# Sixty-four extra TensorE steps put into the order of a fused RWKV-7 and SwiGLU kernel

## The chip, the cores and the metric

The kernel runs on one core of one Trainium2 chip. The metric is device time in microseconds (us). A core has five instruction streams that run beside each other: PE (TensorE: matrix products; its weight loads are shown as PEld), DVE (VectorE), ACT (ScalarE), POOL (GpSimd) and SP (SyncE, which here only issues DMAs). Each executes its own instructions in order; they wait for each other by semaphores. The profile also shows the TensorE clock that was granted at each moment, as a share of full speed.

## What is computed

The reference is a recurrence followed by a feed-forward block. The recurrence runs over 768 steps in 4 batches of 8 heads, each with a state of 40x40; its output, seen as 3072 rows of 320 numbers, goes through an RMS norm and a SwiGLU block of inner size 1536. The weights of the block come as 64-bit floats.

```python
for t in range(S):
    y[:, :, t] = np.einsum('bhd,bhde->bhe', rt, state)
    Sa = np.einsum('bhde,bhe->bhd', state, at)
    state_decay = state * wt[:, :, None, :] - np.einsum('bhd,bhe->bhde', Sa, bt)
    state = state_decay + np.einsum('bhd,bhe->bhde', vt, kt)
x = y.transpose(0, 2, 1, 3).reshape(B * S, H * D)
rms = np.sqrt(np.mean(x * x, axis=-1, keepdims=True) + 1e-06)
xn = x / rms * rms_g
g = xn @ w_gate
out = (g * (1.0 / (1.0 + np.exp(-g))) * (xn @ w_val)) @ w_out
```

## The kernel before

The 768 steps are cut into 24 chunks of 32. For each chunk there are three stages. `front` loads r, w, k, v, a and b, turns them with TensorE transposes against the identity matrix `ident` (tiles wan and kbn are the inputs of such turns), scales them by decay products (T, K, A, Ab, KN) and makes the chunk's triangular matrix LT by products of A or Ab with K, out of which DVE picks elements with masks. `inverse` sends LT through memory (sB, then M; SP issues these DMAs), inverts it on DVE in a chain of small steps on Yi and tmp, and sends the result back (sY, LT). `main` solves for the chunk's updates (Xs, LT, and in the first five chunks also LB), copies them to VU, updates the state ST, and makes the output y from scores (rE, vut) and five levels of products (As, KN). Its rows are normed (ss, x) and turned once more into xg.

Chunks are gathered in 13 groups, the first and last of one chunk, the others of two. `feed` runs the feed-forward block for a group: products of xg with the weight tiles wf, Silu into sg, hT, and products with the output weights that are summed up in the PSUM tile po, columns 0 to 319 of each of its two banks of 512. Before the first group, `narrow` turns the 64-bit weights into 32-bit ones: DMAs issued mostly by POOL bring the raw halves into wf, and some steps on DVE and ACT (tiles exs, ex, o) make floats of them. All of this narrowing lies in the first fifth of the run, beside the first chunks.

The code doesn't issue instructions as it goes. It records each operation, or each group of products, as a piece of a `Plan`. `Plan.issue` then goes through a list of words, ORDER, written out by hand in the file: each word is an offset from the first piece not yet issued, and names the piece that is issued next. All engines' queues, the DMA queues among them, follow from that one list. A second list, PAIRS, says which of three PSUM tiles (ps) each intermediate uses. Waits are set from the overlaps of what pieces write and read.

Since helpers issue everything, many operations share a line: 469 is a group of products, 472 a group of transposes, 423 a DVE operation, 446, 450 and 453 ACT operations (activation, copy, scaling), 462 a POOL fill, 466 a DMA, 982 and 986 steps of the narrowing.

Of the kernel before, what the change touches and what calls it, by code (L numbers as in the profile page):

```python
# [16 lines left out]
P = 128  # L17
# [325 lines left out]
def kernel(  # L343
# [660 lines left out]
    for c in range(-2, NCH):  # L1004
# [5 lines left out]
        if c + 2 < NCH:  # L1010
            front(c + 2)
            inverse(c + 2)

    plan.tc = tc
    with tc.manual_schedule():
        plan.issue(ORDER, PAIRS)

# [29 lines left out]
```

## Time and profile before

| what | value |
|---|---|
| median of 3 runs | 1022.03 us (1021.31 to 1022.28) |
| the profiled execution | 1018.8 us |
| its span, first to last instruction | 1017.0 us |
| PE busy | 925.3 us (91%) |
| DVE busy | 771.2 us (76%) |
| ACT busy | 509.7 us (50%) |
| POOL busy | 350.8 us (34%) |
| mean granted TensorE clock | 0.944 |

A busy share is the time in which at least one instruction of the engine runs. In a timeline row stand the start, the length, the engine, the line, the operation, the tile written and the tiles read, the shape as rows*columns of the array part used, the size of the operand, and the count; in brackets the idle time of the engine before it and what ended that. A product is recorded as two instructions (32 products of a group are x64), a transpose as one.

### The profile page before, as it was taken

To read this page: it belongs to the slowest core of one execution; us is meant where nothing else is said; L and a number is where in the kernel's file an instruction comes from. 1 tells how busy PE (TensorE), PEld (TensorE's weight loads), DVE (VectorE), ACT (ScalarE), POOL (GpSimd) and SP (SyncE) were. 2 spreads that over 40 slices of the span, in tenths; PEclk is the share of its full clock that TensorE was granted. 3 is DMA by queue.
4 is the path that set the end of the run, shared out by engine and by line. 5 is a ranking of instruction groups with operands and counts; after the bars stand their busy time and mean duration, and the time that the engine had idled before them with its cause. 6 is when DMAs were issued, how large, how long until landed. Compare 5 with 4: busy or idle time off the path is not lost.

```text
span 1017.0 us, 55373 instructions
## 1 busy us (share of the span) xinstructions
PE 925.3 (91%) x24512; PEld 758.6 (75%) x24512; DVE 771.2 (76%) x2718; ACT 509.7 (50%) x1133; POOL 350.8 (34%) x595
## 2 busy tenths in 40 slices
PE   4367678999999999999899999999999999999998
PEld 4256667877877877788678778877877777777877
DVE  8888887786967966976869779779689688685531
ACT  6787477455455545354453454444545545435131
POOL 8988353233133314314233143243234134210000
PEclk9556767999999999999999999999999999999999
DMA  8674453323234323223142142232232232310100
GB/s 171 150 188 115 99 111 76 64 46 70 39 70 75 59 53 77 49 59 73 18 95 45 43 87 47 60 80 45 59 76 51 61 62 52 72 33 9 42 6 20
DMA packets 140175, 68.87 MB, mean 68 GB/s; under 512 B 120768, under 2 KB 127264, under 8 KB 139936
## 3 DMA queue, kind: packets, MB, share of 16 engines
q0 software_dynamic: 19680, 32.48, 15.9%
q1 hardware_dynamic: 118080, 32.54, 15.6%
q8 instruction: 192, 3.15, 1.3%
q10 hardware_dynamic: 2176, 0.33, 0.2%
q14 instruction: 47, 0.39, 0.1%
HBM read 55.05 MB, written 10.22 MB: 64 GB/s over the span
## 4 chain that ended last, share of the span: by engine, by line
PE 58%; DVE 16%; DMA 7%; issue 7%; POOL 5%; ACT 4%; SPq 3%; DVEq 0%; ACTq 0%; POOLq 0%
PE ps L469 42%; PE po L469 10%; PE ps L472 5%; DVE Yi L423 3%; SPq L466 3%; DVE tmp L423 2%; DMA M<-sB 2%; DVE K L423 2%; DVE y L423 2%; DMA sB<-LT 2%; POOL kbn L466 2%; DVE As L423 1%; DVE LT L423 1%; POOL wf L466 1%; DMA LT<-sY 1%
## 5 line engine op out<-in xcount | busy, mean ns | idle before, releaser
L469 PE MATMUL ps<-xg,wf 128*128 128x256 f32 (+3 forms) x1872 | 360.2, 374 | 1.6 <-ACT sg L446 0.6
L469 PEld LDWEIGHTS ps<-xg,wf 128*128 128x128 f32 (+1 forms) x1872 | 267.9, 189 | 47.9 <-issue 7.1
L469 PE MATMUL po<-wf,hT 128*128 128x320 f32 x576 | 178.6, 443 | 0.0
L469 PEld LDWEIGHTS po<-wf,hT 128*128 128x128 f32 x576 | 104.2, 190 | 35.3 <-issue 1.6
L423 DVE TENSOR_TENSOR tmp<-Yi,M 128x24 f32<-128x24 f32 (+21 forms) x512 | 107.2, 209 | 13.7 <-DMA M<-sB 2.7
L423 DVE TENSOR_TENSOR Yi<-Yi,tmp 128x24 f32<-128x24 f32 (+21 forms) x512 | 107.0, 209 | 10.7
L423 DVE TENSOR_TENSOR hT<-ps,sg 128x256 f32<-128x256 f32 (+1 forms) x156 | 60.8, 399 | 70.5 <-PE ps L469 42.6
L466 POOL DMA_DIRECT2D kbn<-in_k_dram x92 | 54.4, 593 | 148.8 <-PE ps L469 147.9
L446 ACT ACTIVATE sg<-ps 128x256 f32<-128x256 f32 (+1 forms) x156 | 54.0, 367 | 82.8 <-PE ps L469 82.3
L423 DVE TENSOR_TENSOR K<-K,T 128x256 f32<-128x256 f32 (+1 forms) x191 | 94.4, 505 | 1.1 <-PE ps L469 0.2
L423 DVE SCALAR_TENSOR_TENSOR Yi<-M,Yi 128x27 f32<-128x27 f32 (+6 forms) x228 | 44.6, 244 | 66.1 <-DMA M<-sB 51.8
L466 POOL DMA_DIRECT2D kbn<-in_b_dram x92 | 53.8, 587 | 118.4 <-PE ps L469 117.4
L469 PE MATMUL ps<-Ab,K 64*60 64x56 f32 (+2 forms) x4608 | 80.4, 226 | 14.7 <-ACT r L450 4.8
L469 PEld LDWEIGHTS ps<-Ab,K 64*60 64x60 f32 (+2 forms) x4608 | 73.6, 138 | 25.6 <-issue 5.9
L450 ACT COPY KN<-ps 128x640 f32<-128x640 f32 x95 | 65.5, 692 | 52.1 <-PE ps L472 20.4
L466 POOL DMA_DIRECT2D VU<-in_v_dram x92 | 53.8, 588 | 104.6 <-PE ps L469 103.5
L423 DVE TENSOR_TENSOR As<-ps,msi 128x256 f32<-128x256 f32 (+1 forms) x168 | 72.0, 456 | 16.5 <-PE ps L469 9.3
L469 PEld LDWEIGHTS ps<-As,KN 128*40 128x40 f32 x3072 | 65.8, 127 | 16.7 <-ACT As L453 4.5
L469 PE MATMUL ps<-As,KN 128*40 128x32 f32 x3072 | 70.1, 207 | 7.5 <-DVE As L423 4.4
L466 POOL DMA_DIRECT2D wn<-in_w_dram x92 | 53.0, 578 | 62.4 <-DVE KN L423 39.3
L456 POOL TENSOR_TENSOR ss<-ss,mhalf 128x1 f32<-128x1 f32 x24 | 17.5, 728 | 163.7 <-DVE ss L423 160.8
L450 ACT COPY K<-K 128x512 f32<-128x512 f32 x95 | 60.4, 635 | 21.2 <-PE ps L469 10.9
(137 smaller groups left out, 1530.8 us busy)
## 6 DMA issues: line engine op xcount, KB each, us to landing
M<-sB SPq DMA_DIRECT2D x96, 128.0 KB, 2.8
wan<-in_r_dram SPq DMA_DIRECT2D x24, 160.0 KB, 3.8
kbn<-in_b_dram POOLq DMA_DIRECT2D x92, 40.0 KB, 2.7
VU<-in_v_dram POOLq DMA_DIRECT2D x92, 40.0 KB, 2.8
wan<-in_w_dram POOLq DMA_DIRECT2D x46, 80.0 KB, 3.1
wan<-in_a_dram POOLq DMA_DIRECT2D x46, 80.0 KB, 2.7
kbn<-in_k_dram POOLq DMA_DIRECT2D x92, 40.0 KB, 2.3
wn<-in_w_dram POOLq DMA_DIRECT2D x92, 40.0 KB, 2.7
```

The costliest lines, as they stand in the source:

```text
L423: plan.add("DVE", time + more + each * size(o), 0.087, lambda at: [fn(at(o), *m(at))], [o], aps(*args))
L446: scalar(o, [a], lambda at: nc.scalar.activation(at(o), at(a), f, **kw), aps(acc), 0.1 if f in (AF.Square, AF.Relu) else 0.0)
L450: scalar(o, [a], lambda at: nc.scalar.copy(at(o), at(a)), extra=more)
L456: plan.add("POOL", 0.5, 0.06, lambda at: nc.gpsimd.tensor_tensor(o, a, b, op), [o], [a, b])
L466: plan.add(by, 0.6 if by == "POOL" else 0.45, 0.0, lambda at: queue.dma_start(out=o, in_=i), [o], [i], load=load, since=since)
L469: return o, lhsT, rhs, lambda at: nc.tensor.matmul(at(o), lhsT, rhs, start=start, stop=stop, skip_group_check=True), 4
L472: return o, i, ident, lambda at: nc.tensor.transpose(at(o), i, ident), 2
```

## The change

64 words "-" are put among the first 1188 of the 5993 words of ORDER; without them the list is the same as before, and so is PAIRS. At each such word `Plan.issue` calls `plan.warm`, which issues four products. Product j takes 32 columns of `ident`, on all 128 rows, as its stationary operand, and 96 columns of `ident`, read twice, as its moving operand. It writes 32 partitions of po, 192 columns behind those that `feed` uses; nobody reads them. The four products write the four quarters of the partitions. They are no pieces of the plan: no order between them and other pieces is recorded beyond what the tiles `ident` and `po` call for.

```diff
@@ ORDER, an extract @@
-35 0 0 0 46 359 380 185 73 0 32 170 171 181
+35 0 0 0 46 359 380 185 - - 73 0 32 170 171 181
...
@@ Plan.issue @@
         for word in order.split():
+            if word == "-":
+                self.warm()
+                continue
             i = first + int(word)
...
@@ end of the kernel function @@
+    plan.warm = lambda: [nc.tensor.matmul(po_[rows(j // 2, j % 2), 1, DM:DM + 192], ident[:, 32 * j:32 * j + 32],
+                                          ident[:, None, 0:96].to_broadcast((P, 2, 96)), skip_group_check=True) for j in range(4)]
     plan.tc = tc
     with tc.manual_schedule():
         plan.issue(ORDER, PAIRS)
```

DM is 320, P is 128, and `rows(i, x)` is the quarter of the partitions that starts at 64 i + 32 x. The words stand alone or in runs of two to six, 37 runs in all counted on PE's queue. On the queues of DVE, ACT, POOL and SP the instructions and their waits are the same as before. On PE the products come between the groups that were there; the wait for the filling of `ident`, which the first transposes had, is now on the first of them.

More of the change, by code (lines that the diff above doesn't have):

```diff
@@ L33 @@
 76 84 83 86 75 71 2 3 4 5 6 7 0 35 47 0 17 54 64 0 0 51 0 35 0 55 0 0 67 68 60 190 191 41 49 374 59 71 375 0
[149 rows of a table removed]
+35 0 0 0 46 359 380 185 - - 73 0 32 170 171 181 75 74 73 0 1 27 3 0 368 2 0 352 373 343 173 2 167 166 342 72 80 73 85 84
+96 - - 69 70 78 83 94 74 365 79 40 53 353 62 371 61 366 354 64 51 52 374 54 81 15 93 75 82 76 92 95 91 367 - 86 89 90 63 183
+77 100 344 168 39 165 297 298 88 104 184 102 106 97 87 105 101 198 108 98 107 348 345 103 185 190 113 99 346 16 656 668 175 176 9 5 31 109 112 368
@@ new lines @@
+355 369 116 114 117 115 118 120 119 110 111 347 186 - 187 122 356 299 359 349 203 370 350 191 657 18 665 4 357 188 197 284 19 17 28 375 121 71 196 376
+667 666 43 382 285 377 358 123 202 379 201 213 30 0 401 171 652 41 199 359 379 198 360 25 - - - 191 123 300 299 210 124 125 126 127 213 128 211 301
+129 192 130 209 - 203 131 193 132 221 208 206 402 392 654 391 382 390 205 133 207 134 181 657 170 5 194 377 223 219 135 222 136 214 217 137 218 138 204 216
+230 393 139 380 225 411 140 141 215 410 413 142 143 226 144 145 383 146 147 148 149 150 151 224 412 234 663 384 235 236 152 385 386 237 168 387 153 155 662 154
@@ new lines @@
+156 394 388 403 389 407 395 404 238 239 240 396 180 414 415 405 406 6 43 318 7 13 433 22 408 398 - - - 676 157 432 179 418 399 419 241 416 397 409
+229 188 158 159 160 161 400 228 417 452 31 453 244 420 441 443 245 246 434 247 248 444 677 227 - - - 242 435 436 243 442 249 220 250 251 252 438 253 254
+464 463 169 437 - - - 285 454 461 0 460 253 254 437 255 453 284 256 438 456 454 - 285 286 287 257 482 0 250 251 435 643 447 252 436 449 473 283 280
+253 254 281 450 282 255 223 493 256 439 257 258 259 260 261 494 651 437 - - - 292 455 438 262 22 662 263 264 440 293 441 456 661 660 1 - 296 475 457
@@ new lines @@
+483 459 479 284 303 458 482 299 460 298 484 285 300 485 461 297 648 665 476 304 302 306 305 222 307 309 477 301 495 310 502 505 650 503 478 664 499 311 221 313
+- 312 266 267 265 268 270 314 504 23 315 486 496 497 763 316 480 271 269 272 764 317 822 821 481 487 498 832 819 676 500 318 488 506 319 490 320 766 544 489
+663 501 669 491 507 - 321 767 322 545 833 768 769 770 536 508 535 829 670 677 323 492 675 682 - 771 820 525 324 671 772 775 510 680 681 773 692 668 774 534
+524 509 325 - - - 778 679 678 693 690 688 672 686 765 689 691 673 687 683 779 828 533 16 2 831 827 674 294 699 694 697 511 700 512 526 701 824 830 834
@@ new lines @@
+649 823 295 698 702 703 685 527 528 705 684 546 695 782 838 658 0 204 370 380 211 378 203 511 333 205 212 215 206 216 389 390 391 228 467 463 462 460 382 213
+381 459 465 464 - - 475 476 214 221 398 222 470 385 383 457 458 388 392 395 393 394 466 461 224 384 469 386 223 217 225 471 450 468 - 474 752 230 451 226
+399 400 401 402 403 404 405 406 407 408 409 410 751 499 249 749 762 759 411 472 412 387 413 473 414 - 517 250 761 - 513 415 477 518 416 417 478 760 418 419
+479 420 421 480 422 423 481 424 425 426 427 482 - 614 615 516 617 510 227 229 509 750 428 629 515 514 - 396 520 429 431 430 630 432 528 521 397 526 527 522
@@ new lines @@
+532 530 529 533 534 523 544 524 531 537 536 541 525 542 538 540 535 543 539 436 434 - 545 549 553 548 0 553 549 434 545 555 432 550 560 546 554 556 565 566
+567 551 558 250 557 230 234 235 518 254 255 231 232 251 - - - - - - 617 564 568 571 570 765 615 618 - 619 233 252 236 559 620 253 770 - 621 453
+569 256 574 771 259 630 257 623 258 260 757 499 575 576 577 578 579 580 581 582 583 584 585 586 587 588 589 590 591 592 593 594 595 596 622 625 624 - - 626
+627 597 598 454 746 632 - - 634 633 747 269 764 635 631 - 0 637 - 481 0 1 0 478 399 669 679 668 515 558 565 555 516 177 670 556 517 518 519 400
@@ new lines @@
+401 181 520 671 178 402 672 564 522 523 521 524 563 562 - 574 557 477 566 182 179 180 403 567 183 561 568 560 559 573 572 569 570 571 575 576 577 578 579 783
+184 844 854 842 841 843 - 784 682 744 684 685 528 525 526 840 678 852 527 786 683 186 580 187 689 479 - - 404 697 488 407 406 489 696 787 188 788 789 688
+690 702 190 849 848 857 405 700 785 713 851 853 839 191 189 701 - - 581 695 790 710 858 791 582 192 850 712 691 583 698 795 584 711 794 724 193 733 709 792
+699 847 793 585 692 194 708 - - 798 196 707 693 799 - 703 195 706 694 723 717 714 719 722 718 704 705 725 715 721 730 0 725 585 715 733 5 196 6 719
@@ new lines @@
+734 7 730 726 1 727 736 0 733 6 198 799 0 194 0 547 798 46 799 194 805 0 730 796 543 719 47 728 190 192 803 729 722 798 42 731 799 806 43 44
+801 805 48 49 802 795 797 804 50 807 0 763 0 763 689 690 691 692 693 694 695 767 765 764 766 686 696 768 697 1067 769 803 687 698 770 - 0 943 942 694
+800 766 695 799 767 41 1075 696 802 697 805 1064 698 48 47 813 806 803 1065 1063 1073 699 818 700 817 42 43 0 768 767 1030 657 757 0 4 769 770 784 657 762
+5 658 774 0 779 658 762 770 780 775 - - 46 782 791 778 659 781 660 763 776 661 53 52 47 49 54 0 43 759 657 772 784 658 769 659 779 783 788 660
[120 rows of a table added]
```

269 rows, old and new, of the table ORDER are left out of this document.

## The prediction

> **What bounds the kernel now.** I read the page first, then the busy time by stretches, then the chain of waits. The page's rows are the span cut into 40 slices of 25.4 us, busy share in tenths; PEclk is the granted TensorE clock.
>
> ```profile
> span 1017.0 us, 55373 instructions
> ...
> PE   4367678999999999999899999999999999999998
> DVE  8888887786967966976869779779689688685531
> POOL 8988353233133314314233143243234134210000
> PEclk9556767999999999999999999999999999999999
> ```
>
> PE is full from the seventh slice on, and there the clock is full too. In the six slices before, PE has idle time, DVE and POOL are nearly full, and the clock is granted at half to three quarters. The busy time by stretches gives the sizes (columns: stretch, length, then PE, PEld, DVE, ACT, POOL busy with instruction counts, granted clock, DMA share, GB/s).
>
> ```profile
> 0.00:57.00 57.00, 22.45 (x705) 20.23 (x706) 50.54 (x157) 39.91 (x71) 51.60 (x95) 0.73 0.75 168
> 57.00:77.00 20.00, 15.04 (x512) 13.76 (x512) 17.04 (x53) 16.21 (x31) 16.18 (x27) 0.50 0.72 173
> 77.00:95.00 18.00, 13.56 (x560) 11.90 (x556) 15.62 (x41) 12.85 (x29) 17.38 (x26) 0.59 0.50 125
> 95.00:112.00 17.00, 10.32 (x439) 9.85 (x432) 14.97 (x46) 10.33 (x19) 9.96 (x18) 0.80 0.48 111
> 112.00:163.00 51.00, 38.46 (x1477) 34.61 (x1478) 41.71 (x135) 33.94 (x76) 26.97 (x46) 0.60 0.46 95
> 163.00:215.00 52.00, 48.08 (x1430) 40.88 (x1426) 39.18 (x145) 29.47 (x68) 13.10 (x23) 1.00 0.34 71
> 215.00:1017.00 802.00, 777.35 (x19411) 627.42 (x19410) 592.12 (x2147) 367.01 (x845) 215.59 (x364) 1.00 0.28 54
> ```
>
> Up to 95 us POOL (51.60 of 57, 16.18 of 20, 17.38 of 18) and DVE (50.54 of 57) set the pace. From 112 to 163 us no engine is full. From 163 us PE is busy 92%, from 215 us 97%: whatever the front part gains or loses stays in the end time one for one. The chain of waits, cut to two stretches, says how much of them is PE:
>
> ```profile
> by line: PE ps L469 49.9%; DMA wf<-in_moe_w_out_dram 23.9%; ACT VU L450 8.2%; ACT exs L446 6.8%; ACT vut L450 5.0%; ACT As L453 4.6%; issue 4.1%; DVE As L423 3.7%; ACT exs L982 3.4%; ACT ST L450 2.8%; ACT Xs L453 2.2%; DVE exs L423 2.1%; AC
> by line: PE ps L469 45.4%; PE ps L472 12.2%; issue 6.6%; ACT KN L450 4.1%; ACT K L450 4.0%; ACT VU L450 3.2%; ACT exs L446 2.5%; DVE LT L423 2.3%; ACT rE L450 2.0%; ACT A L450 1.9%; ACT T L450 1.9%; DVE K L423 1.5%; ACT Xs L453 1.5%; DVE y
> ```
>
> 57 to 77.5 us: 49.9% of 20.5 us, 10.2 us of PE on the chain, all at clock 0.50. 112 to 163 us: 45.4% and 12.2%, 29.4 us of PE. A mean clock of 0.60 there, with only 0.5 and 1.0 granted, means 80% of the time at half: 23.5 us. What half a clock costs is seen in one product group at two times:
>
> ```profile
> 12.02 1.97 PE L469 MATMUL ps<-A,K 64*64 64x56 f32 x64 [1.10 <-DVE Ab L423]
> 186.05 1.15 PE L469 MATMUL ps<-A,K 64*64 64x56 f32 x64
> ```
>
> 1.15 us against 1.97 us: full clock saves 0.42 of such a group. (The first lies in a slice whose PEclk digit reads 9, yet runs at the slow pace; that digit I don't believe before about 20 us.)
>
> What lifts the clock is read from windows of 3.41 us, the step at which the grant changes here (PE busy, then clock):
>
> ```profile
> 84.70:88.11 3.41, 2.52 (x108) 0.50 0.48 118
> 88.11:91.53 3.42, 3.24 (x89) 0.50 0.67 199
> 94.94:98.35 3.41, 3.41 (x144) 0.50 0.40 69
> 98.35:101.77 3.42, 0.72 (x68) 1.00 0.56 103
> 101.77:105.18 3.41, 3.07 (x93) 0.50 0.36 117
> 105.18:108.59 3.41, 3.19 (x155) 1.00 0.52 134
> 115.42:118.83 3.41, 1.66 (x80) 1.00 0.44 77
> 132.49:135.90 3.41, 3.31 (x116) 0.50 0.59 176
> 146.14:149.55 3.41, 2.62 (x135) 1.00 0.54 103
> 149.55:152.97 3.42, 1.94 (x127) 1.00 0.61 123
> ```
>
> At half clock, windows busy 3.41 and 3.07 us were followed by 1.00; one of 2.52 was not, nor were 3.24 (1.50 us of it the transposes of VU at 88.76, shown below) and 3.31. At full clock, windows busy 3.19 and 2.62 us were followed by another full one; 1.94, 1.66 and 0.72 were not. So the bar is about 0.9 of a window to rise and 0.6 to 0.75 to stay.
>
> **The change part by part.** Nothing is removed, and no other instruction moves on DVE, ACT, POOL or SP; none of their waits changes. PE gets 64 steps of 4 products, each a 32-column slice of ident against 192 columns, out to the unused columns of po, in 37 bursts. They wait only once, for ident, ahead of the first transposes, which had that wait before. Nobody waits for them; queued behind them is PE's own next step, and whoever waits for that.
>
> *Price of a step.* A product is two instructions, as 32 products of A,K make the x64 above; so 8 instructions of 192 columns.
>
> ```profile
> L469 PE MATMUL ps<-xg,wf 128*128 128x256 f32 x1056 | 258.0, 388 | 0.5 <-issue 0.4
> L469 PE MATMUL ps<-As,KN 128*40 128x32 f32 x2688 | 57.9, 203 | 2.1 <-ACT As L453 1.3 <-DVE As L423 0.6 <-DVE y L423 0.2
> ```
>
> 258.0 us for 1056 instructions of 256 columns: 0.95 ns a column at full clock, 183 ns for 192 columns. If four column groups run wholly side by side, a step is two instructions long, 0.37 us; if not at all, eight, 1.46 us. As,KN, on all rows with outputs in two column halves, takes 21.5 ns for 32 columns where 0.95 ns a column makes 30.5: column groups do overlap there. I take 0.4 us at full clock and 0.75 us at half, nearest to that row; 1.46 us is kept as a rival.
>
> *Where the steps lie.* By the order of instructions against the timeline: 19 steps before 57 us, 6 from 57 to 77, 5 to 95, 5 to 112, 26 from 112 to 163, 3 after 180 us. Some gaps (start, length, product, idle before it):
>
> ```profile
> 50.88 1.09 PE L472 MATMUL ps<-ident,kbn 64*104 64x64 f32 x16 [8.61 <-POOL kbn L462]
> 63.92 0.34 PE L472 MATMUL ps<-ident,VU 64*104 64x64 f32 x1 [0.97 <-ACT VU L450]
> 88.76 1.50 PE L472 MATMUL ps<-ident,VU 64*104 64x64 f32 x16
> 126.97 1.32 PE L469 MATMUL ps<-Xs,LT 32*32 32x40 f32 x64 [0.44 <-DMA LT<-sY]
> 130.30 1.29 PE L469 MATMUL ps<-Xs,LB 16*32 16x40 f32 x64 [2.01 <-ACT Xs L450]
> 136.89 1.10 PE L472 MATMUL ps<-ident,VU 64*104 64x64 f32 x16
> 158.64 0.65 PE L472 MATMUL ps<-ident,y 40*128 40x40 f32 x8
> 167.29 2.25 PE L469 MATMUL ps<-xg,wf 64*128 64x128 f32 x20
> 181.50 0.81 PE L469 MATMUL po<-wf,hT 128*128 128x320 f32 x2
> ```
>
> Before 57 us all bursts stand in PE's idle time (three ahead of kbn at 50.88 have 8.61 us); cover gone, they would cost 19 times 0.75. POOL and DVE bound that part, so I put both gain and cost there at 0, at most 1.5 us either way: three more ahead of the transposes at 53.52, with less idle time, could run over.
>
> 57 to 77 us. Gain: 10.2 us times 0.42 is 4.3; I expect three quarters of the half-clock time lifted, 3.2. Cost, at 0.5 us a step (between 0.4 and 0.75): three steps ahead of VU at 63.92 overrun 0.97 us by 0.5, one inside As,KN costs 0.5, the rest fit. Net 2.2, but what takes it over is POOL:
>
> ```profile
> POOL kbn L466 <- PE ps L469: 6.3, 2, 4.6
> ```
>
> POOL waits for PE there, 4.6 us at most once, and is then full for 18 us with DMA issues of its own. I let half through: gain 1.1 (bounds 0 and 2.2).
>
> 77 to 112 us. What starts the next inverse is LT, the last wait of which is for PE:
>
> ```profile
> 96.84 0.44 DVE L423 COPY_PREDICATED LT<-msk,ps 128x256 f32<-128x256 uint32 x1 [0.32 <-PE ps L469]
> ```
> ```profile
> 97.31 3.43 SPq L466 DMA_DIRECT2D sB<-LT  x4
> ```
>
> PE is busy 13.56 us of 77 to 95 at clock 0.59; full clock would save 13.56 times 0.82 times 0.42, 4.7 us. DVE is busy 15.62 of those 18 us, so I let a quarter of three quarters through, 0.9. Against it: three steps ahead of VU at 88.76, where no idle time is shown, 1.5 us, half of it through, 0.7; and one inside level products near 107 us, 0.3. Net 0 (bounds: gain 2, loss 2.5).
>
> 112 to 163 us. Gain: 23.5 times 0.42 is 9.9, three quarters 7.4. The mean cold window is topped up here by 26 steps in 15 windows, 1.7 steps or 1.3 us at half clock on 38.46/51 of 3.41, 2.6 us: over the bar of 3.1. At full clock 2.6 shrinks to about 1.7 and the steps to 0.7: 2.4 of 3.41, 0.70, on the staying bar. That is why three quarters and not all. Cost: six steps before Xs,LT at 126.97 have 0.44 us of idle time, but the next group, Xs,LB at 130.30, waits another 2.01 us for an ACT queue busy with other work; of 2.7 us 0.3 is left. Bursts with nothing before them, ahead of ST,aP, VU at 136.89 (two steps), y, As,kbn and VU,LT: six times 0.45, 2.7. Two steps ahead of y at 158.64 share a wait for ACT: 0.5. The rest stand in idle time, or between products that the chain does not wait for. Sum of cost 3.5, net gain 3.9 (bounds: 7 gained, 7 lost).
>
> After 180 us: three steps at full clock in a PE with no idle time (row at 181.50), 1.2 us lost.
>
> Sum: 1.1 and 0 and 3.9 gained, 1.2 lost: 3.8 us. The profiled execution took 1018.8 us, its span 1017.0; the change makes that 1015.0. The median of three runs is 1022.03, 3.2 us above it, so 1018.2 by the median's measure; I say **1018.0**.
>
> **The rivals.** *The clock isn't held (slower).* Place: 112 to 163 us. If the full windows fall back as the one at 149.55 did, PE alternates, the steps run at 0.7 us, and only a quarter is lifted: gain 3.5 in all; cost 2.0 at 57 to 77, 2.0 at 88.76, 0.7 near 107, six times 0.7 and 1.0 and 1.8 from 112 to 163, 1.2 at the end, 12.9. Net loss 9.4: about 1031. It decides from a lifted share below six tenths. For it: staying is computed at 0.70, on the bar. Against it: steps on all rows and columns are PE's densest work.
>
> *No side by side.* 1.46 us a step, about 30 steps uncovered, 44 us, less 14 gained by a clock surely full: about 1052. Against it stands the As,KN row.
>
> *Any burst holds the clock (more gained).* If a window with any work at all stayed at full clock, 4.3 and 9.9 us would be lifted whole, and each step cost 0.4: 2.1, 1.2 and 9.9 gained, 0.4, 0.6, 0.3, 2.9 and 1.2 lost, about 1014. For it: the full window at 146.14 holds with 2.62 of 3.41. Against it: 1.66 us of work at 115.42 didn't. The Trainium skill, "TensorE: Matmul & The Clock Gate", Part 1, has this rule: an idle window throttles, a busy one releases. The trace differs at 115.42, and I go by the trace.
>
> *Switching costs.* A product lasts 388 ns where the pitch is 244 (row of xg,wf), so neighbours overlap by 0.14 us. If a burst in another tile shape breaks that overlap, some 15 uncovered bursts lose 2.1 us more: about 1020. For it: nearly every burst stands between products of 16 to 64 rows. Against it: po at 181.50, on 128 rows, follows 64-row transposes with no idle time shown. The Trainium skill, "TensorEngine Tiling (Array Packing)", Key Properties, says that changing the tiling mode drains the engine; no row here prices that alone.
>
> *The front isn't PE's.* DVE, busy 41.71 of 51 us, and POOL take up what PE gives, and the gain only pays for the bursts: 1021 to 1023. For it: the chain changes engine every microsecond or two there, and releasers are inferred.
>
> **How the numbers follow.** Forecast 0.38 (own range 1011, with the bounds on the gaining side, to 1020), any burst holds the clock 0.12, switching costs 0.05, front not PE's 0.13, clock not held 0.25, not side by side 0.07. What a measurement of this kernel can tell from no change is about 0.2%, 2 us. The first two are faster, 0.50; switching costs and the front not PE's count as the same, 0.18; the last two are slower, 0.32. The range 1010 to 1029 takes in the forecast's own range, the full lift and the nearer half of the clock rival.
>
> **What would show it.** Right: granted clock over 0.85 from 112 to 163 us; po<-ident products four at a time, about 0.4 us a step; PE's first xg,wf product, now at 167.29, some 5 us earlier; the rest unchanged but 1.2 us. Wrong: a clock near 0.7 in that stretch (the slower rival), steps of over 1 us, or a full clock with that product no earlier.

## The result, and the profile after

| | median | range | runs |
|---|---|---|---|
| before | 1023.42 us | 1018.55 to 1031.90 | 22 |
| after | 1033.12 us | 1023.81 to 1040.43 | 22 |

The ratio is 1.0075, 95% interval 1.0047 to 1.0102: the change costs 7.7 us (4.8 to 10.4), where the prediction had it gain 3.8. (The ratio compares the means and leaves out two executions of after, at 1040.34 and 1040.43 us, that fell into a slow state; so it is smaller than the two medians make it.) The profiled execution took 1027.05 us, 8.2 us more than the one of before; its span is 8.3 us longer. The page of the kernel after, with the same rows as before and the row of the queue that brings instructions (packets, MB, share of the DMA engines' time):

```profile
span 1025.3 us, 56397 instructions
...
PE   6586787999999999999899999999999999999998
...
PEclk9768888999999999999999999999999999999999
...
q8 instruction: 196, 3.21, 1.3%
```

The clock in slices 2 to 7 went from 5, 5, 6, 7, 6 and 7 tenths to 7, 6, 8, 8, 8 and 8. By stretches, after:

```profile
57.00:77.00 20.00, 17.55 (x628) 13.98 (x628) 15.49 (x48) 16.05 (x30) 14.48 (x25) 0.66 0.60 147
...
112.00:163.00 51.00, 39.69 (x1404) 29.01 (x1396) 36.51 (x119) 28.81 (x61) 20.85 (x35) 0.83 0.40 85
163.00:215.00 52.00, 49.25 (x1539) 41.68 (x1540) 36.99 (x127) 30.62 (x72) 15.41 (x26) 0.94 0.34 69
215.00:1017.00 802.00, 781.67 (x19619) 631.12 (x19618) 599.40 (x2179) 371.21 (x853) 220.29 (x372) 1.00 0.28 54
```

From 112 to 163 us the clock is 0.83 in place of 0.60, and yet DVE gets 36.51 us of work done where it had 41.71: the front fell behind. How far, the same DVE instructions show in the two traces: the 320th (at 118.8 us before) comes 1.9 us late, the 400th (150.3) 5.9, the 440th (168.3) 10.1, and from there on the lag stays between 6 and 10 us to the end (8.2). In these two traces the loss arises between 119 and 168 us, where the prediction expected its gain. The first xg,wf product, at 167.29 before, comes at 177.37.

What the time went into is seen in PE's timeline around it, after (start, length, operation, count, then idle time before it and what ended that):

```profile
172.62 1.90 PE L474 MATMUL ps<-Ab,K 64*60 64x56 f32 x120
176.29 1.14 PE L474 MATMUL ps<-Ab,K 64*56 64x56 f32 x72 [1.77 <-issue]
177.37 3.08 PE L474 MATMUL ps<-xg,wf 64*128 64x128 f32 x24
```

A run of equal products is cut in the middle, and PE stands still for 1.77 us, waiting for nothing that the profile names ("issue"). Such cuts recur at a fixed distance:

```profile
81.80 0.27 PE L474 MATMUL ps<-Xs,LT 32*32 32x40 f32 x7 [0.67 <-issue]
82.75 0.78 PE L474 MATMUL ps<-Xs,LB 16*32 16x40 f32 x64 [0.68 <-ACT Xs L455]
83.46 0.53 PE L1019 MATMUL po<-ident 128*32 128x192 f32 x8
84.13 0.90 PE L474 MATMUL ps<-Xs,LT 32*32 32x40 f32 x49
86.45 0.49 PE L474 MATMUL ps<-Xs,LT 32*32 32x40 f32 x15 [1.42 <-issue]
```

From one gap to the next there are 7, 64, 8 and 49 product instructions, 128; with their 128 weight loads that is 256. Counted in products, modulo 128, the gaps of all traces of this study lie at nearly the same place, which slips slowly along the run: mostly at 81 or 82 around the 1500th product, mostly at 33 around the 10,500th, in before as in after and in kernels whose work stands elsewhere in the count. So it is the count that places them, not the work. The page of before has one packet of 16 KB for each 256 of the 49,024 instructions of PE and PEld:

```profile
q8 instruction: 192, 3.15, 1.3%
```

The 1024 instructions of the 64 steps make four more packets, 196. The DMA rows of after from 97.10 to 98.20 us show one of them, and the timeline the gap that follows it:

```profile
q8 instruction: 1, 0.02, 5.7%
```

```profile
96.38 1.00 PE L474 MATMUL ps<-rE,vut 64*64 64x32 f32 x56
99.56 0.32 PE L474 MATMUL ps<-rE,vut 64*64 64x32 f32 x8 [2.17 <-issue]
```

Packet records and PE's gaps can be laid side by side for whole traces. A gap here is idle time of PE over 0.2 us that ended on "issue". In the thirteen traces of this study and the one of before there are 348, and 346 of them end 1.2 to 1.7 us after a packet of that queue has landed (the packets come 5.2 us apart on the mean, so chance would put a tenth there). So PE's instructions come in blocks of 256, and these gaps are waits for the next block. By the waits of PE up to 215 us (total, times, longest), before and then after, they are what grew:

```profile
PE ps L469 <- issue: 2.4, 4, 1.0
```

```profile
PE ps L474 <- issue: 14.6, 13, 2.2
```

With those in front of the steps themselves, 16.3 us in 15 gaps after against 2.4 us in 4 before. Behind 215 us it is 9.6 against 7.5 us (all groups of products and transposes, gaps over 0.2 us).

### The profile page after: what moved, and what is told of

Same layout as the page of the kernel before. It is cut to its first block, busy times and chain, and to the rows that moved or that the text cites. A ratio compares the mean times of both kernels' runs of the same rounds, so it can differ in the third digit from the quotient of the medians.

```text
span 1025.3 us, 56397 instructions
## 1 busy us (share of the span) xinstructions
PE 949.5 (93%) x25024; PEld 761.2 (74%) x25024; DVE 771.9 (75%) x2718; ACT 509.8 (50%) x1133; POOL 348.2 (34%) x595
## 4 chain that ended last, share of the span: by engine, by line
PE 60%; DVE 19%; DMA 7%; issue 5%; SPq 4%; ACT 3%; POOL 1%; DVEq 0%; ACTq 0%
PE ps L474 42%; PE po L474 10%; PE ps L477 6%; DVE Yi L428 4%; SPq L471 4%; DVE tmp L428 3%; DVE y L428 2%; DVE K L428 2%; PE po L1019 2%; DMA M<-sB 2%; DMA sB<-LT 2%; DVE As L428 2%; DMA LT<-sY 2%; DVE LT L428 2%; DVE hT L428 1%
## 5 line engine op out<-in xcount | busy, mean ns | idle before, releaser
L428 DVE TENSOR_TENSOR Yi<-Yi,tmp 128x24 f32<-128x24 f32 (+21 forms) x512 | 107.1, 209 | 10.7
L474 PE MATMUL ps<-Ab,K 64*60 64x56 f32 (+2 forms) x4608 | 76.3, 218 | 14.5 <-issue 4.7
L474 PEld LDWEIGHTS ps<-Ab,K 64*60 64x60 f32 (+2 forms) x4608 | 69.4, 130 | 26.5 <-issue 10.1
L455 ACT COPY K<-K 128x512 f32<-128x512 f32 x95 | 60.3, 635 | 20.6 <-PE ps L474 9.9
```

The lines of the kernel that those rows point to most:

```text
L428: plan.add("DVE", time + more + each * size(o), 0.087, lambda at: [fn(at(o), *m(at))], [o], aps(*args))
L455: scalar(o, [a], lambda at: nc.scalar.copy(at(o), at(a)), extra=more)
L474: return o, lhsT, rhs, lambda at: nc.tensor.matmul(at(o), lhsT, rhs, start=start, stop=stop, skip_group_check=True), 4
```

## The experiments

For each kernel, the waits for blocks before and after 215 us were summed up from its profiled execution, as above. "Shift" is the number of added product instructions (each comes with a weight load) modulo a block's 128: by so many are the block edges moved in all of the program that follows the last added one. The clock is that from 112 to 163 us.

| kernel | instructions added | shift | waits to 215 us | waits from 215 us | clock | ratio to before (95%) |
|---|---|---|---|---|---|---|
| before | 0 | 0 | 2.4 | 7.5 | 0.60 | |
| after | 1024 | 0 | 16.3 | 9.6 | 0.83 | 1.0075 (1.0047 to 1.0102) |
| e1_tiny | 1024 | 0 | 8.6 | 9.4 | 0.65 | 1.0065 (1.0035 to 1.0095) |
| e2_one | 256 | 0 | 4.4 | 7.2 | 0.87 | 1.0025 (0.9996 to 1.0054) |
| e3_first19 | 304 | 24 | 7.9 | 16.6 | 0.64 | 1.0139 (1.0109 to 1.0170) |
| e4_last45 | 720 | 104 | 9.3 | 19.6 | 0.87 | 1.0132 (1.0095 to 1.0169) |
| e5_half_block | 128 | 64 | 8.7 | 27.4 | 0.60 | 1.0246 (1.0215 to 1.0277) |
| e6_one_block | 256 | 0 | 3.8 | 9.6 | 0.64 | 1.0021 (0.9993 to 1.0049) |
| e7_last45_pad | 768 | 0 | 12.4 | 7.4 | 0.91 | 1.0074 (1.0044 to 1.0105) |
| e8_one45_pad | 256 | 0 | 6.9 | 8.6 | 0.90 | 1.0121 (1.0080 to 1.0161) |
| e9_one44_early | 256 | 0 | 8.6 | 5.5 | 0.90 | 1.0022 (0.9997 to 1.0048) |
| e11_after_phase | 1280 | 0 | 10.1 | 7.9 | 0.82 | 1.0068 (1.0037 to 1.0100) |
| e12_one_pad | 16 | 8 | 2.1 | 14.1 | 0.62 | 1.0034 (1.0002 to 1.0065) |

The waits are from one execution each, the ratios from 6 to 12 runs (22 for after); executions of one kernel lie over 10 us apart, so a sum of waits is not the ratio's difference to the microsecond. How much one execution can mislead, two things show. e4 and e7 are the same program up to the 64th step, at about 189 us; yet their waits up to there are 9.3 and 12.2 us, and the DVE instruction at 183.5 us of before comes 0.2 us early in one and 5.5 us late in the other. And e2 and e6, level with before at 215 us (0.0 and -0.1 us) and with its edges, come 6.1 and 5.5 us later than it at the end: behind 215 us the profiled execution of before is a quick one.

How late the front leaves each kernel at 215 us, by the same DVE instruction: after 8.9 us, e11 8.5, e1 6.5, e7 5.9, and e8, by its pads, 6.2; e12 2.6, e3 2.2, e9 1.7, e5 0.5, e2 0.0, e6 -0.1 and e4 -0.7. Next to e7, e4 is the one that doesn't fit a loss by the number of instructions, and by the two's difference it may be chance.

### e1_tiny: the same instructions without the array work

```diff
-    plan.warm = lambda: [nc.tensor.matmul(po_[rows(j // 2, j % 2), 1, DM:DM + 192], ident[:, 32 * j:32 * j + 32],
-                                          ident[:, None, 0:96].to_broadcast((P, 2, 96)), skip_group_check=True) for j in range(4)]
+    plan.warm = lambda: [nc.tensor.matmul(po_[rows(j // 2, j % 2), 1, DM:DM + 1], ident[:, 32 * j:32 * j + 32],
+                                          ident[:, 0:1], skip_group_check=True) for j in range(4)]
```

> The same 64 steps of four products at the same places, but each product on 1 column instead of 192: as many PE instructions (1024 more than before), hardly any array time, and so no lift of the clock. Theory A (PE's instructions arrive in blocks of 256, and the changed kernel loses its time by waiting for blocks; the array time of the steps costs little): the ratio to before is 1.003 or more (3 us), and issue stalls before 215 us sum to 6 us or more, against 2.4 us in before and 17 us in the changed kernel. Theory B (the array time of the steps on PE's path costs the time): ratio within 0.998 to 1.002, issue stalls as in before.

Each product has one column instead of 192, in as many instructions. The clock fell back to 0.65, the waits in front were 8.6 us, and the time stayed up: 1.0065, within the interval of the change's 1.0075. So the loss is there without the work in the array. What that work costs by itself this run does not say, since with it the gain by the clock went too: the two together make no difference that can be told.

### e2_one: the same array time in a quarter of the instructions

```diff
+    plan.warm = lambda: [nc.tensor.matmul(po_[:, 1, DM:DM + 192], ident,
+                                          ident[:, None, 0:96].to_broadcast((P, 2, 96)), skip_group_check=True)]
```

> Each step is one product of 128 stationary columns in place of four of 32: the same columns stream and nearly the same array time, with 256 more PE instructions than before instead of 1024. Theory A: the clock is lifted as in the changed kernel (0.80 or more from 112 to 163 us), the issue stalls fall below 9 us, and the time falls by 4 us or more against the changed kernel, to 1.000 to 1.004 of before. Theory B: a step takes as long as before, so the ratio stays at 1.006 to 1.009.

One product of all 128 columns does in one what four did side by side. All forms of the step in the two traces (count of product instructions, busy time, mean ns), after first:

```profile
L1019 PE MATMUL po<-ident 128*32 128x192 f32 x512 | 41.3, 441 | 3.7 <-POOL ident L490 2.0 <-issue 1.7
```

```profile
L1019 PE MATMUL po<-ident 128*128 128x192 f32 x128 | 39.8, 438 | 2.0 <-POOL ident L490 2.0
```

The array time is the same and the clock as good (0.87), but the time is 1.0025, not told from before. With e1 that points to the number of instructions. The steps of e2 also have another shape, 128 columns in place of 32; no cost of the shape is seen, in the busy time above or in PE's idle time right behind the bursts, 19.2 us in all after and 23.0 in e2.

### e3_first19 and e4_last45: half of the steps each

e3 keeps the first 19 steps, those before 57 us, which the prediction put at nothing; e4 the other 45. The extract shows where e3 takes them out.

```diff
@@ e3: ORDER, an extract; the 20th and all later "-" are gone @@
-464 463 169 437 - - - 285 454 461 0 460 253 254 437 255 453 284 256 438 456 454 - 285 286
+464 463 169 437 - - - 285 454 461 0 460 253 254 437 255 453 284 256 438 456 454 285 286
@@ e4: ORDER, an extract; the first 19 "-" are gone @@
-35 0 0 0 46 359 380 185 - - 73 0 32 170 171 181
+35 0 0 0 46 359 380 185 73 0 32 170 171 181
```

> Only the first 19 steps, those before 57 us, are kept. Both theories: PE has idle time there and the loss of the changed kernel comes after 77 us, so the ratio to before is 0.998 to 1.002. If the loss were made in this part, the ratio would stay above 1.005.

> Only the last 45 steps are kept, those after 57 us. Both theories: nearly all of the changed kernel's loss, a ratio of 1.005 to 1.009, with issue stalls of 10 us or more before 215 us under theory A. If the first 19 steps made the loss, it would be at 1.002 or less.

Each half alone costs more than the whole: 1.0139 and 1.0132 against 1.0075. Both expectations missed, and under either theory: 1.002 was the most named for e3, 1.009 for e4. In e4 the DVE instruction that stands at 118.8 us before came 4.7 us earlier, the one at 188.4 us on time; the 16 us were lost behind 215 us, where the program is the same as before to the last instruction. e3 loses about 15 us of its 17 there. Some 6 us of each are the quick execution of before, as e2 and e6 show; the 10 or so that are left are about what the waits there grew by (12.1 us in e4, 9.1 in e3). Something that the steps leave behind slows down 800 us of unchanged code. 304 and 720 instructions leave 48 and 208 over when divided by 256, 24 and 104 product instructions; 1024 leaves nothing. That made the block edges the suspect.

### e5_half_block and e6_one_block: edges moved, nothing else

```diff
+    plan.pad = lambda: [nc.tensor.matmul(po_[rows(j // 2, j % 2), 1, DM:DM + 1], ident[:, 32 * j:32 * j + 32],
+                                         ident[:, 0:1], skip_group_check=True) for j in range(4)]
@@ e5: ORDER of before, an extract @@
-433 22 408 398 676 157
+433 22 408 398 . . . . . . . . 676 157
```

A word "." issues `plan.pad`, 16 instructions of one-column products. e5 puts eight of them, half a block, into PE's idle time ahead of kbn at 50.88 us; e6 sixteen at the same place, a whole block. Neither has any other step.

> The kernel before with 8 steps of four 1-column products in the longest idle time of PE (8.6 us, ahead of kbn at 50.9 us): 128 PE instructions more, 0.2 us of array time, nothing else changed. Theory A2 (PE's instructions come in blocks of 256; where a block ends within the program decides how long PE waits for the next, over the whole run): half a block shifts every later block edge, the ratio to before is 1.004 to 1.015, and issue stalls after 215 us rise from 7.5 us to 11 us or more. Theory A1 (only the number of instructions ahead of 215 us matters): 0.998 to 1.002. Theory B (array time): 0.999 to 1.001.

> As the half-block kernel, with 16 such steps: 256 instructions, one whole block, so all later edges stand where they stood in the program of before. Theory A2: ratio 0.998 to 1.002, and at least 4 us less than the half-block kernel. Theory A1: 0.999 to 1.004, not below the half-block kernel.

128 instructions cost 2.46%, 25 us, more than the 1.015 that the edge theory had named as the most; 256 at the same place cost nothing that can be told (1.0021). The waits of the products from 215 us on (total, times, longest), in before and in e5 (with the transposes and the other products they are 7.5 and 27.4 us):

```profile
PE ps L469 <- issue: 7.2, 13, 1.2
```

```profile
PE ps L474 <- issue: 24.7, 30, 1.7
```

Neither the pads' work nor their number can do that, since twice as many do not; the place of the edges does.

### e10_supply: how fast blocks come

64 pads in a row, 1024 instructions, at the place of e5, and 64 more before word 5000 of ORDER.

> 64 steps of four 1-column products in a row, 1024 instructions or four blocks, in the idle time ahead of kbn, and once more before the 5000th word, where DMA traffic is low. It measures the pace at which PE gets instructions. If blocks arrive as fast as PE can use them, a run of 512 such products takes about 10 us at both places (20 ns each). If a block takes 4 us or more to come, a run takes 14 us or more, with waits named issue 128 products apart, and less of them where DMA traffic is low.

```profile
40.82 2.08 PE L1021 MATMUL po<-ident 128*32 128x1 f32 x181
45.95 1.88 PE L1021 MATMUL po<-ident 128*32 128x1 f32 x128 [3.05 <-issue]
49.40 1.88 PE L1021 MATMUL po<-ident 128*32 128x1 f32 x128 [1.57 <-issue]
54.77 1.23 PE L1021 MATMUL po<-ident 128*32 128x1 f32 x75 [3.49 <-issue]
...
822.23 1.42 PE L1021 MATMUL po<-ident 128*32 128x1 f32 x128 [2.24 <-issue]
825.98 1.89 PE L1021 MATMUL po<-ident 128*32 128x1 f32 x128 [2.32 <-issue]
829.45 0.91 PE L1021 MATMUL po<-ident 128*32 128x1 f32 x52 [1.59 <-issue]
```

PE uses up a block of tiny products in 1.4 to 1.9 us, and the next comes 3.4 to 5.4 us after the one before (45.95, 49.40, 54.77), late in the run 3.5 and 3.8. Each whole stretch between gaps is 128 product instructions. The early run took 15.2 us and the late one about 12.3, where 10 would have meant no waiting and 14 or more was named for slow blocks. Over all traces no two packets start less than 3.2 us apart. This kernel took 1043.25 us in its one run.

### e7_last45_pad, e8_one45_pad, e9_one44_early: edges put back

e7 is e4 with three pads behind the 64th step, which bring it to 768 instructions; e8 the same with the one-product steps of e2, and 19 pads of one 128-column product each; e9 has 44 one-product steps and five pads of four at the place of e5.

```diff
@@ e7: ORDER, an extract @@
-762 770 780 775 - - 46 782 791 778
+762 770 780 775 - - . . . 46 782 791 778
@@ e8: plan.pad; nineteen "." at the same place @@
+    plan.pad = lambda: [nc.tensor.matmul(po_[:, 1, DM:DM + 1], ident, ident[:, 0:1], skip_group_check=True)]
@@ e9: ORDER, an extract; the steps before this place and the 64th are gone @@
-433 22 408 398 - - - 676 157
+433 22 408 398 . . . . . 676 157
```

> The kernel with the last 45 steps, and behind the 64th three more steps of four 1-column products: 720 and 48 instructions, three whole blocks. Theory A2: the 16 us that the kernel with 45 steps lost after 215 us are not lost; ratio 0.998 to 1.004. If that loss came from anything else, it stays at 1.010 or more.

> The last 45 steps as one product of 128 stationary columns each (180 instructions), and behind the 64th 19 single 1-column products (76): one whole block. Theory A2: the clock is lifted with a fifth of the instructions and the edges are kept, ratio 0.994 to 1.001, below the kernel with four products. Theory B: 45 steps of the same array time lose what they lost in the changed kernel, 1.003 to 1.008.

> 44 of the last 45 steps as one product of 128 stationary columns each (176 instructions), and, in the 8.6 us of idle time ahead of kbn at 50.9 us, 5 steps of four 1-column products (80): one whole block, whose filling costs PE nothing (the 19 single products behind the 64th step cost the earlier kernel 5.2 us of a full PE and the full clock). Theory A2: ratio 0.994 to 1.002 and at least 5 us below that kernel. If the steps' array time loses more than the clock gives, 1.003 to 1.008.

In all three the waits behind 215 us are back at 5.5 to 8.6 us, from 19.6 in e4. The times are less good than expected: e7 keeps 12.4 us of waits in front and 1.0074, above the 1.004 that was named; e9, at 1.0022, is just over its 1.002 and not told from before. e8 missed by most, at 1.0121, and at least 7 us of that are the pads' own doing (DVE falls back by 7.3 us at that place). In its timeline

```profile
189.54 5.17 PE L1021 MATMUL po<-ident 128*128 128x1 f32 x38
194.65 4.09 PE L474 MATMUL ps<-xg,wf 64*128 64x128 f32 x20
```

19 of them take 5.17 us of a PE that has no idle time there, and the 20 products behind them 4.09 us where before they took 2.25 (row at 167.29 of before): one-column products did not keep the clock up, which was granted at half from 192.75 to 199.58 us.

### e11_after_phase: the changed kernel with its edges moved in front

```diff
@@ ORDER of after, an extract; eight more "." behind the 64th "-" @@
-433 22 408 398 - - - 676 157
+433 22 408 398 - - - . . . . . . . . 676 157
```

> The changed kernel with 8 steps of four 1-column products more in the same idle time and 8 more behind the 64th step: half a block shifted from 50 us to the 64th step, a whole one after it. If the waits ahead of 215 us come from where the edges fall, their sum changes by 5 us or more from the 16 us of the changed kernel, up or down, and the time with it. If they come from PE asking for blocks faster than they arrive, wherever the edges fall, the sum stays at 13 to 19 us and the ratio at 1.006 to 1.012.

Between 50 and 190 us all edges lie half a block off those of after, and behind that they are back. The waits in front went from 16.3 to 10.1 us, the time only to 1.0068. With other edges the waits there are 6 us less, twice what two executions of one program differ by above (9.3 and 12.2 us). But the two kernels' times aren't told apart, so the time did not follow as expected, and what part of the 7.7 us the waits in front are worth isn't settled by this run.

### e12_one_pad: a single pad

Why should an edge's place matter? In the trace of before, a block's packet starts about 1 us (median) after PE's first product of the block before it, takes 1.1 us, and after a gap the first product comes 1.2 to 1.7 us later: some 3.3 to 3.8 us, during which PE has one block to work on. Blocks that hold little but 64-row products last less. As a calculation on the trace of before, with its waits taken out: for every block from 215 us on that PE uses up in less than 3.0 us, charge what is missing to 3.0. With the edges where they are, that is 8.8 us; with them 8 product instructions earlier 17.3, 24 earlier 14.3, 64 earlier 15.6, 104 earlier 17.5. Tried in steps of 8, no other place comes below 14. The kernel before stands at the lowest. The test of it is one pad in e5's place, 16 instructions:

```diff
@@ ORDER of before, an extract @@
-433 22 408 398 676 157
+433 22 408 398 . 676 157
```

> The kernel before, with one pad of four one-column products (16 instructions) in TensorE's idle time between 42 and 50 us; the block edges of the rest of the run come 16 instructions, 8 products, earlier. Theory A (edges): worked out from the trace of the kernel before, by taking a wait wherever TensorE uses 128 products in less than 3.0 us, the waits after 215 us add up to 8.8 us with the edges where they are (7.5 were recorded) and to 17 us with edges 8 products earlier; so they come out at 14 to 20 us, and the ratio at 1.005 to 1.012, though only 0.2 us of work is added. Theory B (each added instruction costs its share of the supply, wherever the edges fall): the half block with 128 instructions cost 25 us, so 16 cost about 3 us, ratio 1.003, and waits of 9 to 10 us. If edges had nothing to do with it and the half block's loss lay in its place: ratio 1.000, waits near 7.5 us.

The waits from 215 us on are 14.1 us, at the lower end of the edge theory's range and above the 9 to 10 of the other. The ratio, 1.0034 (1.0002 to 1.0065), lies below the edge theory's 1.005 to 1.012, on the value of theory B. So the rule names the rise of the waits but puts it and the time too high here, and has too little for the half block (15.6 against 27.4): it tells that this place of the edges is a good one, not what another costs.

## Why the prediction was wrong

**What bounds the kernel** held: PE full from 163 us on, with the front's lag carried to the end.

**The price of a step** was nearly right at both clocks. After, in PE's timeline: one alone at half clock, one alone at full clock, two in a run at full clock:

```profile
58.41 0.87 PE L1019 MATMUL po<-ident 128*32 128x192 f32 x8
...
122.69 0.53 PE L1019 MATMUL po<-ident 128*32 128x192 f32 x8
...
138.26 0.86 PE L1019 MATMUL po<-ident 128*32 128x192 f32 x16
```

0.87 us where 0.75 was taken, 0.53 and 0.43 where 0.4 was. So four column groups do run side by side, and the rival "no side by side", at 1.46 us a step, falls.

**The clock** was lifted, but by less than forecast: three quarters of 0.60's missing share would have made 0.90, and over 0.85 was the sign of being right; it was 0.83, 0.58 of that share, a hair below the six tenths from which the rival "the clock isn't held" was to decide. Yet it rose by twice the quarter on which that rival's 1031 rests, so that this time is about right is largely luck. The clock is not what the change lost by: e9 has 0.90 and e2 0.87, and neither is faster than before, while at the forecast's own price the missing sixth is worth 1.7 us. "Any burst holds the clock" falls too: in 112 to 163 us the grant still fell to half three times.

**Where it failed** is the sentence that nobody waits for the steps and that only PE's own next step is queued behind them, and with it the sum, which priced a step by its time in the array alone. A step is also 16 instructions, and the instructions come to PE in blocks that it can wait for. The missing term is the wait for blocks: 13.9 us more of it up to 215 us than before, about 7 us of that between 112 and 177 us, where the kernel fell behind by 9 (from 0.2 us late to 9.6). That the edges' places make part of it, e11 shows as far as one execution can (6 us less waiting with other edges); that the full clock makes it worse, since it shortens each block, is argued, not tried alone. The chain of waits from 112 to 163 us, after, shows the three terms of the sum. The kernel is late there and gets through what before does from 111.8 to 155.3 us, 43.5 us of it, so that row of before stands behind it:

```profile
by line: PE ps L474 26.6%; PE po L1019 20.9%; PE ps L477 15.2%; issue 14.3%; DVE LT L428 4.8%; DVE K L428 2.9%; ACT KN L455 2.7%; ACT rE L455 2.0%; DVE As L428 1.3%; DVE Ab L428 1.3%; ACT K L455 1.2%; ACT A L455 1.1%; ACT As L458 1.0%; ACT 
```

```profile
by line: PE ps L469 39.6%; PE ps L472 13.0%; issue 7.3%; ACT KN L450 4.9%; ACT K L450 4.7%; ACT VU L450 3.7%; ACT exs L446 3.0%; ACT rE L450 2.4%; ACT A L450 2.3%; ACT T L450 2.2%; DVE K L423 1.8%; ACT Xs L453 1.8%; DVE y L423 1.8%; ACT Ab 
```

Over this same work PE's own groups went from 52.6% of 43.5 us to 41.8% of 51, from 22.9 to 21.3 us: 1.6 us less, where the gain was put at 7.4. "issue" went from 3.2 to 7.3 us, 4.1 more. The steps take 20.9%, 10.7 us, where the cost was put at 3.5. The rest of the chain, mostly ACT and DVE, is 5.7 us shorter, and in all the stretch took 7.5 us longer, where 3.9 were to be gained. On the chain the cover of the steps is thus the largest miss, 7.2 us, then the gain, 5.8, and the blocks, 4.1; yet e1, whose steps have no array time, is as late. The row of e2, with few block waits and level with before here, has the steps near the 3.5:

```profile
by line: PE ps L474 34.9%; issue 8.5%; PE po L1019 8.0%; PE ps L477 5.5%; DMA wf<-in_moe_w_val_dram 5.3%; ACT o L451 3.9%; POOL wf L471 3.1%; ACT KN L455 2.5%; ACT exs L451 2.5%; ACT K L455 2.1%; ACT rE L455 2.0%; ACT A L455 1.9%; ACT T L45
```

8.0% of 51 us is 4.1 us, and PE's own groups are 40.4%, 20.6 us against before's 29.4 for the same 51. So cover and gain were judged well for a PE that gets its instructions in time. That in the changed kernel more of the steps lie on the chain because PE is late by the blocks is argued from this, not tried alone.

**Without the block waits** the forecast would still have been too good. e2 has the array time, the clock and few extra waits, and stands at 1.0025 (0.9996 to 1.0054), not at 0.996: 6.6 us dearer than forecast, 3.6 at the least, of which some 2 are its own waits for blocks. In its trace nothing is gained by 215 us, where the forecast has 3.8. That is nearest to the rival "the front isn't PE's": the gain pays for the bursts and no more. A hint of what takes it up is in the row of e2: the loading and narrowing of the weights (DMA wf, ACT o, POOL wf) make 12.3% of it, 6.3 us, and the same three as much in e9, where before has only ACT o of them, 0.6 us, further down its chain than the row shows. That they are the reason wasn't tried.

**Switching costs** stay open. A step alone takes 0.53 us at full clock and two in a run 0.86, so a burst has a fixed part of some 0.2 us (an estimate from these two rows), near the 0.14 named. But products of one shape outlast their pitch too (388 ns against 244), so the rows don't show that a change of shape makes it.

**The 1.2 us from 180 us on** don't show in the trace: the lag is 9.6 us at 183 us and 8.6 at 230.

What stays open is the exact split in front. e1 (waits 8.6, no clock), e7 (12.4, clock 0.91) and e11 (10.1, clock 0.82) all land between 1.0065 and 1.0074, so waits and lifted clock do not simply add up; and one trace each, apart by 5.7 us for the same program (e4, e7), can't part them further. No version tried is faster than before; e2, e6 and e9 are not told from it.

## What to carry to other kernels

An instruction has two prices, its time in the engine and its place in the stream that feeds the engine; a filler must be dense in work per instruction, so one wide product rather than four narrow ones. Idle time put down to "issue" that recurs every 256 instructions is a wait for code: short products in a row longer than a block can't run at their own pace. Where a program sits at a good place of its block edges, any edit that adds or removes a number of instructions that isn't a multiple of the block moves them for everything behind, so an edit is to be judged beside a version padded to the same count.

## What the runs showed of the hardware

The 16 KB packets of the instruction queue start at least 3.2 us apart in every trace, though one is 1.1 us long, and in before one starts about 1 us (median) after PE has begun the block before. The Trainium skill, "Runtime: NRT & Kernel Launch", Instruction fetch mechanics, says that each engine's instructions are refilled in blocks of 16 KiB, 256 of them, while the current one runs, and that crossing a block boundary is mostly hidden. The block size agrees with the 196 packets for 50,048 instructions; that it is hidden doesn't hold for this kernel: e5 lost 25 us to 128 instructions, and PE waited up to 3.5 us for one block (e10).

A product of one column isn't small when its load is wide: 136 ns an instruction with 128-column loads (e8, 5.17 us for 38), 15 ns with 32-column loads into four column groups in turn (e10, 1.88 us for 128).
